# B transposed by the DMA engines, the state drive of chunk 0 moved behind its gate/up stage, and the down projections put behind the outputs of the chunk ahead, in a fused S5 and SwiGLU kernel

## The chip, the cores and the metric

One Trainium2 chip, one core of it. The metric is the device time of one execution in microseconds (us). Lower is better. A kernel is called faster or slower from 2% on.

Names of engines: PE is TensorE, PEld its weight loads, DVE is VectorE, ACT is ScalarE, POOL is GpSimd and SP is SyncE. A "q" behind a name (ACTq, SPq) marks a DMA issue in that engine's queue. L12 is line 12 of the kernel at hand, so that the same function has different line numbers in different kernels.

## The reference

The input is x of 2048 tokens by 448 features in bf16. A layer norm feeds two branches: a linear recurrence with 448 complex states (S5), and a SwiGLU feed-forward of width 1792. The output joins them.

```python
def _A_ref(x, Lambda_re, Lambda_im, B_re, B_im, C_re, C_im, log_dt, Dskip):
    Lam = Lambda_re + 1j * Lambda_im
    Lam_bar = jnp.exp(jnp.exp(log_dt) * Lam)
    B_bar = ((Lam_bar - 1.0) / Lam)[:, None] * (B_re + 1j * B_im)
    Bu = jnp.einsum("bld,pd->blp", x + 0j, B_bar)
    # h[t] = Lam_bar * h[t-1] + Bu[t], for 2048 steps
    return 2.0 * jnp.einsum("blp,dp->bld", hseq, Cmat).real + x * Dskip

def _B_ref(x, w_gate, w_up, w_down):
    return (silu(x @ w_gate) * (x @ w_up)) @ w_down

xn = _layernorm(x)
out = x + _A_ref(xn, ...) * silu(_B_ref(xn, w_gate, w_up, w_down))
```

## The kernel before

The tokens go through in four chunks of 512 (W), each of four tiles of 128 (TQ). One chunk needs, in this order of dependence:

- **drive**: bu = xn times B (PE), then a row of DVE steps. They turn bu against the phase tables CT and ST, scan each state over time, and turn back. The results are H_re and H_im.
- **gate/up** (`gu`): 14 blocks of 128 columns of the two weight matrices, two blocks at a time. ACT empties each PSUM bank, DVE multiplies, and the product is Vt.
- **downs**: four down projections (PE), each followed by a silu on ACT, which gives `sg`.
- **outs**: four output sums y = H times C (PE), which DVE multiplies by sg and adds to x.

The DVE steps of the drive are put in a background list. `bg.run(budget)` issues a few of them, and `bg.finish(q)` issues all that are left of chunk q. In the traces ACT and DVE run their instructions in the order in which the program issues them (the prediction shows an `sg` held up to 68.32 us behind four copies), so these calls decide what stands ahead of what.

```python
def b_transpose(c, d, eng):              # B is loaded as it lies, then turned on PE
    tp = bank("tpb", BF16).rearrange("p (i w) -> p i w", i=2)
    for i in range(2):
        for k in (KF, *range(KF)):
            ...
            nc.tensor.transpose(tp[:, i, c0 : c0 + P], nat[:, c, k, blk(d + i)], Id[:])
    ...                                   # and copied to BT by ACT or DVE

def bu(q, ns, packed=False):              # products with B; ACT empties the banks
    ...
    if packed:                            # swaps the halves of the packed last block:
        turn_over(b1[:, KF, :], b0[:, KF, :])   # two copies of 64 x 512 on ACT

def c_weights(k):                         # scales C by the factors of B_bar: block k
    ...
    for i, (o, ho, u, v) in enumerate(to):
        nc.scalar.activation(tb, natC[h, 1, k, :], ACT.Copy, scale=v[h, k : k + 1])
        nc.vector.scalar_tensor_tensor(out=C2[ho, o, :], in0=natC[h, 0, k, :],
            scalar=u[h, k : k + 1], in1=tb, op0=ALU.mult, op1=ALU.subtract)

def ssm_steps(bg, q):                     # DVE: 6 steps, 7 scans, then
    ...
    step(KF, h1, b1, CT, ALU.mult); step(KF, "t", b0, ST, ALU.mult)
    step(KF, h1, h1, "t", ALU.add)
    step(KT, h0, b0, CT, ALU.mult); step(KT, "t", b1, ST, ALU.mult)
    step(KT, h0, h0, "t", ALU.subtract)   # the last one completes H_re
```

The order of the stages (hooks: what is issued behind the n-th pair of gate/up blocks):

```python
load_w(nc.sync, nc.sync, Wg, B_w_gate, 0, C0)     # C0 = 256
load_w(nc.scalar, nc.scalar, Wu, B_w_up, 0, C0)   # two loads issued by ACT
load_nat(0, A_B_re)
...
gu(0, bg, 2.0, {
    0: [*stats(4, 5, 6, 7), *sqrt(1), on(params_in), on(table_phase, 0)],
    1: [*bs(1), *rstd_of(1), *norms(4, 5, 6, 7), on(table_sin, 0)],
    2: [*transposes(4, 5, 6, 7), on(load_c), on(table_phase, 1), on(table_sin, 1),
        on(bu, 0, (0, 1)), on(table_phase, 2), on(table_sin, 2)],
    3: [on(bu, 0, (2,), True), on(table_phase, 3), on(table_sin, 3), on(params_fold)],
    4: [on(params_trig), on(ssm_steps, bg, 0)],
    5: [on(params_out)],
}, begun)
gu(1, bg, 0.9, {
    1: stats(8, 9),
    2: [*stats(10, 11), *sqrt(2), on(c_weights, 0)],
    3: [*rstd_of(2), *norms(8, 9), on(c_weights, 1)],
    4: [*norms(10, 11), *transposes(8, 9), on(c_weights, 2)],
    5: [*transposes(10, 11), on(c_weights, 3)],
})
drive(1, 4.8)
for q in range(NQ - 1):
    # downs(q) with bg.run(2.2) after each; bg.finish(q); outs(q)
    # then, where there is a chunk q+2: drive(q+2), gu(q+2)
    ...
```

## Time and profile before

| | before |
|---|---|
| median of 3 runs | 190.0 us |
| span of the profiled execution | 188.1 us |
| busy: PE, DVE, ACT | 97%, 85%, 56% |
| first gate/up matmul | 7.40 us |
| downs of chunk 0 begin (S in what follows) | 64.30 us |
| first output sum of chunk 0 (first y matmul) | 74.90 us |
| last step of H_re of chunk 0, start and duration | 71.18 us, 1.23 us |

The page cuts the span into 40 equal slices, here 4.7 us each. Each digit is a busy share in tenths; in the row PEclk it is the TensorE clock that was granted, in tenths of full speed. These are two rows of the kernel before:

```profile
DVE  4889995899999999989999899789369999789253
PEclk9999999999999999999999999999999999999999
```

The clock is at full speed throughout. DVE is nearly full from the eighth to the 25th slice, among others with the drive's steps, and has some room after that. PE's own row is in the prediction.

### The profile page before, as it was taken

The numbers are of one execution on the slowest core, as the hardware profiler recorded it, in microseconds if no ns is written. First come the engines' busy times: TensorE is split into PE (matmuls) and PEld (weight loads), VectorE is DVE, ScalarE is ACT, GpSimd is POOL, SyncE is SP. The second block draws the span as 40 slices with busy tenths as digits, with TensorE's granted clock in tenths as the row PEclk, the third lists the DMA queues.
The fourth block names the chain that finished last, engine by engine and source line by source line (L and its number), as shares of the span: only waits on it lengthen the run. The fifth ranks groups of instructions, "written<-read, shape, count | busy, mean of one in ns | idle before, by whom it ended". The sixth has DMA issues, their size and how long they took to land.

```text
span 188.1 us, 3787 instructions
## 1 busy us (share of the span) xinstructions
PE 182.1 (97%) x1512; PEld 93.9 (50%) x1512; DVE 160.3 (85%) x266; ACT 105.1 (56%) x201; POOL 11.2 (6%) x21
## 2 busy tenths in 40 slices
PE   7799999999999999999999999999999999999992
PEld 2575455555555555545444455545444445555551
DVE  4889995899999999989999899789369999789253
ACT  3278699939999871018878632108977552302100
POOL 6422100000020000000020000000000000000000
PEclk9999999999999999999999999999999999999999
DMA  5999997300012100011004000020000000020020
GB/s 152 340 378 383 378 177 144 74 3 2 3 28 56 31 0 0 0 54 51 0 3 97 14 3 0 3 84 15 2 0 3 0 0 0 3 73 24 0 78 24
DMA packets 21122, 12.61 MB, mean 67 GB/s; under 512 B 11120, under 2 KB 20080, under 8 KB 21104
## 3 DMA queue, kind: packets, MB, share of 16 engines
q1 hardware_dynamic: 20288, 12.05, 23.2%
q10 hardware_dynamic: 688, 0.31, 0.6%
q8 instruction: 12, 0.20, 0.5%
q14 instruction: 6, 0.05, 0.1%
q0 software_dynamic: 128, 0.00, 0.0%
HBM read 8.03 MB, written 1.84 MB: 52 GB/s over the span
## 4 chain that ended last, share of the span: by engine, by line
PE 84%; DVE 9%; ACT 3%; DMA 1%; issue 1%; POOL 0%; SPq 0%; DVEq 0%
PE hd L559 23%; PE gp L424 20%; PE up L424 19%; PE y L574 11%; PE pb L424 9%; PE y L580 2%; DVE st L230 1%; DMA x_all<-in_A_x_dram 1%; DVE xn L248 1%; DVE f L356 1%; DVE a L357 1%; ACT CT L306 1%; DVE Vt L551 1%; ACT bu_im L458 1%; ACT bu_re L458 1%; DVE mv L231 1%
## 5 line engine op out<-in xcount | busy, mean ns | idle before, releaser
L424 PE MATMUL gp<-xT,Wg 64*128 64x512 bf16 (+1 forms) x406 | 86.2, 369 | 0.1
L424 PE MATMUL up<-xT,Wu 64*128 64x512 bf16 (+1 forms) x406 | 85.8, 369 | 0.1
L424 PEld LDWEIGHTS <-Wg 64*128 64x128 bf16 x406 | 36.9, 94 | 23.0 <-issue 1.6
L424 PEld LDWEIGHTS <-Wu 64*128 64x128 bf16 x406 | 37.2, 94 | 20.1 <-POOLq L406 0.3
L559 PE MATMUL hd<-Wd,Vt 128*128 128x448 bf16 x224 | 43.2, 353 | 0.0
L546 ACT ACTIVATE gs<-gp 128x512 bf16<-128x512 f32 x56 | 34.9, 623 | 12.4 <-PE gp L424 9.0
L547 ACT ACTIVATE us<-up 128x512 bf16<-128x512 f32 x56 | 35.2, 629 | 0.0
L559 PEld LDWEIGHTS <-Vt 128*128 128x128 bf16 x224 | 21.7, 98 | 21.0 <-issue 1.1
L564 ACT ACTIVATE sg<-hd 128x448 bf16<-128x448 f32 x16 | 8.7, 544 | 38.2 <-PE hd L559 38.2
L424 PE MATMUL pb<-xT,BT 64*128 64x512 bf16 (+1 forms) x224 | 22.0, 349 | 0.0
L551 DVE TENSOR_TENSOR Vt<-gs,us 128x2048 bf16<-128x2048 bf16 (+1 forms) x16 | 17.3, 1081 | 5.5 <-ACT us L547 5.4
L458 ACT ACTIVATE bu_re<-pb 128x512 bf16<-128x512 f32 (+1 forms) x20 | 10.0, 526 | 18.1 <-PE pb L424 18.1
L590 DVE TENSOR_TENSOR t<-y,sg 128x448 f32<-128x448 f32 (+2 forms) x17 | 10.1, 595 | 10.4 <-PE y L574 10.0
L574 PE MATMUL y<-C,H_re 128*128 128x448 bf16 (+2 forms) x68 | 17.6, 341 | 0.0
L424 PEld LDWEIGHTS <-BT 64*128 64x128 bf16 x224 | 11.2, 94 | 11.0 <-issue 0.7
L494 DVE TENSOR_TENSOR_SCAN bu_re<-rcol,H_re,ere 128x512 bf16<-128x512 f32 x12 | 15.1, 1269 | 0.0
L580 PE MATMUL y<-Dd,xT 128*128 128x128 bf16 x64 | 13.5, 212 | 0.0
L574 PE MATMUL y<-C,H_im 128*128 128x448 bf16 (+2 forms) x51 | 11.9, 342 | 0.0
L494 DVE TENSOR_TENSOR_SCAN bu_im<-rcol,H_im,eim 128x512 bf16<-128x512 f32 x9 | 11.3, 1260 | 0.0
L230 DVE BATCH_NORM_STATS2 st<-x_all 128x6 f32<-128x448 bf16 x16 | 9.9, 616 | 1.6 <-DMA x_all<-in_A_x_dram 1.5
L593 DVE TENSOR_TENSOR ob<-t,x_all 128x448 bf16<-128x448 f32 (+2 forms) x17 | 10.2, 597 | 0.6
L215 POOL TENSOR_TENSOR sd<-vep,halves 128x1 bf16<-128x1 bf16 (+1 forms) x7 | 5.9, 845 | 77.0 <-PE up L424 41.6
(90 smaller groups left out, 166.6 us busy)
## 6 DMA issues: line engine op xcount, KB each, us to landing
out_dram<-ob SPq DMA_DIRECT2D x15, 112.0 KB, 1.7
Wd<-in_B_w_down_dram SPq DMA_DIRECT2D x1, 1568.0 KB, 12.6
x_all<-in_A_x_dram SPq DMA_DIRECT2D x1, 896.0 KB, 14.5
Wg<-in_B_w_gate_dram SPq DMA_DIRECT2D x1, 768.0 KB, 8.2
Wu<-in_B_w_up_dram SPq DMA_DIRECT2D x1, 768.0 KB, 9.3
x_all<-in_A_x_dram SPq DMA_DIRECT2D x1, 448.0 KB, 5.1
Wg<-in_B_w_gate_dram SPq DMA_DIRECT2D x1, 384.0 KB, 4.9
Wu<-in_B_w_up_dram SPq DMA_DIRECT2D x1, 384.0 KB, 5.1
```

Source lines behind the costliest of these rows:

```text
L230: nc.vector.bn_stats(out=st[:], in_=x_all[:, n, :])
L424: mm = nc.tensor.matmul(out, lhsT=w[h, d, :], rhs=xT[h, d, q * W + c0 : q * W + c1], start=(first and m == 0), stop=(not first and m == 3 ...
L458: nc.scalar.activation(to, pair[i][0], ACT.Copy)
L494: nc.vector.tensor_tensor_scan(out=T["b"][c][:, k, :], data0=rcol[:, k : k + 1].to_broadcast([P, W]), data1=T["e"][c][:, k, :], initial=in ...
L546: nc.scalar.activation(gs[:, i + j, :], gp_[:], ACT.Silu)
L547: nc.scalar.activation(us[:, i + j, :], up_[:], ACT.Copy)
L551: nc.vector.tensor_tensor(out=Vt[:, f0 : f0 + n, :], in0=gs[:, 0:n, :], in1=us[:, 0:n, :], op=ALU.mult)
L559: nc.tensor.matmul(hd, lhsT=Vt_of[q][:, fi, j * P : (j + 1) * P], rhs=Wd[:, fi, :], start=(fi == 0), stop=(fi == NF - 1),)
L574: nc.tensor.matmul(y[:, c0:c1], lhsT=h, rhs=C2[:, n, c0:c1], start=(n == 0), stop=(n == NS - 1))
L580: nc.tensor.matmul(y[:, s + skip : s + P], lhsT=xT[:, n, m * P : (m + 1) * P], rhs=Dd[:, n, skip:P], start=False, stop=False,)
L590: nc.vector.tensor_tensor(out=t[:], in0=y, in1=sg[:, c0:c1], op=ALU.mult)
L593: nc.vector.tensor_tensor(out=ob[:], in0=t[:], in1=x_all[:, m, c0:c1], op=ALU.add)
```

## The change

Its intent, as the diff shows it:

1. **B turned by DMAs.** Six transposing loads write BT straight from memory, so the 32 PE transposes and their copies go. The loads wait (an empty instruction on SyncE) until Wu's columns up to 1280 have landed.
2. **Left halves of three blocks first.** The first 256 tokens are multiplied by three gate/up blocks, not two, before the next tokens are transposed. The added columns are loaded early, two of the parts being issued by ACT. DVE, no longer ACT, reads the `up` banks of the first pair.
3. **Drive 0 behind gate/up 0**, where its products with B stood inside gate/up 0 before.
4. **Down projections behind the outputs of the chunk ahead.** For the later chunks gate/up now comes between the downs and the outputs. Half of the scaling of C (blocks 2 and 3) and the layer norm of tiles 8 to 11 move out of gate/up 1 and in among the downs and outputs of chunk 0.
5. A root by the power of -0.5 in place of a power of 0.5 and a reciprocal.

```diff
+    def load_b(landed):
+        gate = nc.sync.nop(nofuse=True)
+        tc.add_manual_dep(gate.ins, landed.ins.name, SYNC, reason="queue")
+        load_turned(BT, A_B_re, 0, D)
+        load_turned(BT, A_B_im[KF * P : D, :], D, R)
+        load_turned(BT, A_B_im[0 : KF * P, :], KT * P, KF * P)
...
-    C0 = 256
+    C0, C1 = 256, 384
...
+    load_w(Wu, B_w_up, 0, C0, nc.scalar)
     load_x(2, TQ)
+    load_w(Wg, B_w_gate, 0, C0)
+    for part in range(2):
+        load_w(Wg, B_w_gate, C0, C1, nc.sync, part)
+        load_w(Wu, B_w_up, C0, C1, nc.scalar, part)
...
+    def second_tokens():
+        ln_evacuate(2, ln_transpose(2), nc.scalar)
+        t = ln_transpose(3)
+        tv = params_row(t)
+        ln_evacuate(3, t, nc.vector)
+        nc.scalar.activation(pcol[:], tv, ACT.Copy)
...
+    first, third = gu_banks(), gu_banks(1)
+    gu_matmuls(0, 0, first, (0, CW))
...
+    gu_matmuls(0, 2, third, (0, CW), between=second_tokens)
...
+    gu(0, bg, 0.0, {
+        0: [*stats(4, 5), on(params_in), on(table_phase, 0)],
+        2: [*stats(6, 7), *root(1), on(table_sin, 0)],
+        3: norms(4, 5, 6, 7),
+        4: [*transposes(4, 5, 6, 7), on(load_rest), on(table_phase, 1)],
+        5: [on(table_sin, 1), on(table_phase, 2)],
+        6: [on(table_sin, 2), on(table_phase, 3), on(params_fold), on(table_sin, 3),
+            on(params_trig)],
+    }, {0: first_pair, 1: second_pair})
+    drive(0, 0.0)
+    gu(1, bg, 1.6, {2: [on(c_weights, 0)], 4: [on(c_weights, 1)]})
     drive(1, 4.8)
...
+    sg = downs(0, 1.4, {
+        0: [on(c_weights, 2)],
+        1: [on(c_weights, 3), *stats(8, 9)],
+        2: [*stats(10, 11), *root(2), run_power],
+    })
+    bg.finish(0)
+    do(norms(8, 9) + transposes(8, 9))
+    outs(0, sg, {1: norms(10, 11) + transposes(10, 11)})
+    sg = downs(1, 2.5)
+    drive(2, 4.8)
+    gu(2, bg, 1.6, {...})
+    bg.finish(1)
+    outs(1, sg)
+    sg = downs(2, 2.5)
+    drive(3, 4.8)
+    gu(3, bg, 2.3)
+    bg.finish(2)
+    outs(2, sg)
...
```

## The prediction

> **What bounds the kernel now.** I read the busy shares first, then the slices.
>
> ```profile
> PE 182.1 (97%) x1512; PEld 93.9 (50%) x1512; DVE 160.3 (85%) x266; ACT 105.1 (56%) x201; POOL 11.2 (6%) x21
> PE   7799999999999999999999999999999999999992
> ```
>
> TensorE (PE) works from the third slice to the last but one, so only work taken off it or waits on it can move the time. Busy time hides short waits; so I went through the timeline by start-to-start distances. From the first real matmul at 7.40 us to the last near 184.5 us nearly every matmul starts when the array is free; all the gaps together are about 2 us. The largest gap, about 0.8 us, lies at 27.6 to 29.3 us, where ScalarE (ACT) was late emptying PSUM banks. The 32 transposes of B stand on PE too (grouped view by shape: columns are line, engine, form, count, then busy us and mean ns).
>
> ```profile
> L371 PE MATMUL tpb<-Id,nat 128*128 128x128 bf16 x32 | 2.1, 219 | 0.0
> L488 DVE TENSOR_TENSOR H_re<-H_re,tmp 128x2048 bf16<-128x2048 bf16 x4 | 4.9, 1224 | 0.1
> L389 DVE SCALAR_TENSOR_TENSOR C<-natC,nb_im,c_tb 128x448 bf16<-128x448 bf16 x3 | 2.0, 680 | 0.0
> ```
>
> They start 62 ns apart: two lots of 16 take 0.99 and 1.00 us. The next view is of the stretch in which the down projections of chunk 0 run, then its outputs (columns: us, then busy us of PE, PEld, VectorE (DVE), ACT, POOL).
>
> ```profile
> 64.30:74.90 10.60, 10.60 (x58) 5.49 (x57) 10.50 (x12) 5.56 (x11) 0.00 (x0) 1.00 0.01 2
> 74.90:81.08 6.18, 6.18 (x45) 3.43 (x45) 6.06 (x7) 0.54 (x1) 0.00 (x0) 1.00 0.00 0
> ```
>
> DVE is full there as well. It is the second engine, and what it delivers, H of chunk 0, is what the outputs read. The timeline shows the margin (start, us, instruction):
>
> ```profile
> 65.75 2.55 ACT L465 ACTIVATE bu_im<-bu_re 64x512 bf16<-64x512 bf16 x4
> 68.32 0.55 ACT L564 ACTIVATE sg<-hd 128x448 bf16<-128x448 f32 x1
> ...
> 71.18 1.23 DVE L488 TENSOR_TENSOR H_re<-H_re,tmp 128x2048 bf16<-128x2048 bf16 x1
> ```
>
> H_re is done at 72.4 us and PE wants it at 74.9: 2.5 us to spare. Note also ACT: the first sg is read only at 68.32, 4.0 us after the downs began, though its sum was ready at 66.95, because four copies of bu stood ahead of it in ACT's queue.
>
> **What the Trainium skill says.** (1) "TensorE: Matmul & The Clock Gate", Back-to-back issue gap: N/2.4 + 2.5 ns when warm. The trace agrees: 56 matmuls of 448 columns in 10.60 us are 189 ns each. (2) The same page, Architectural detail: ACT and DVE queues are strict first in, first out. The late sg above agrees, and my main step rests on it. (3) The same page, Part 1: a TensorE idle for one window of some 3.4 us can fall to half clock, and needs about as long to recover. The trace shows the half rate at the start only (dummy matmuls of 448 columns 0.37 us apart), no fall later, as PE never idles so long. (4) "DMA: Bandwidth & Descriptors", DMA Transpose (X-bar): 2-byte types, from Sync or Scalar, beside ordinary DMAs. Here a transposing load of C took 3.9 us to land, and SyncE some 1.3 us to issue.
>
> **The change, part by part.** I call S the moment at which the down projections of chunk 0 begin (64.3 before). Everything ahead of S first.
>
> - Start. ACT now issues four weight loads ahead of its first evacuation. The compiled order shows the fourth waiting for a DMA semaphore last used by the left 192 KB of Wg. Those landed 4.3 us after their issue at 2.13, so 6.4. The issue takes 0.45, and only then can ACT empty the two transposes of x:
>
> ```profile
> 5.96 0.60 ACT L261 ACTIVATE xT<-tp 128x512 bf16<-128x512 bf16 x1 [3.73 <-PE tp L259]
> 6.76 0.60 ACT L261 ACTIVATE xT<-tp 128x512 bf16<-128x512 bf16 x1 [0.20 <-PE tp L259]
> ```
>
>  They move to about 7.0 and 7.5, and the first matmul from 7.40 to 8.15: **+0.75**. The power of -0.5 saves a reciprocal (0.16) that no longer matters.
> - B by DMA: **-1.99** on PE, the 0.99 and 1.00 above. The six loads wait until Wu's columns up to 1280 have landed, about 14 us; six issues of 1.3 and 3.9 to land give about 26, and they are wanted at about 30.6: hidden.
> - Left half of the third block: no matmul more or less in all. It covers the transposes, but the copy of xT waits behind six parameter transposes in its bank, and the six matmuls left (0.33 us) cover it only in part: **+0.3**.
> - Drive 0 behind gate/up 0: the gap of 27.6 to 29.3 goes, **-0.8**. In its place ACT has the last two tables (1.15 us each, waiting for DVE's phases, 2.4 each) ahead of bu's evacuations. By my walk through both queues the first bank is free 0.65 us after PE wants it for gate/up 1: **+0.65**.
>
> Sum before S: 0.75 - 1.99 + 0.3 - 0.8 + 0.65 = **-1.1**; S is about 63.2.
>
> After S. PE runs four downs, 4 x 2.65 = 10.6 us, then asks for H of chunk 0. The compiled order says what DVE must do first. The third column pair of C stands before the last steps of H, and reads c_tb, which ACT makes behind the first sg. As before, the four copies hold sg to S + 4.0. Then sg 0.5 and c_tb 0.7: S + 5.2. From there DVE has, at start-to-start times of the trace: 4 scalings of C at 0.6 = 2.4; the last H_im step 0.95; LayerNorm statistics of tiles 8 to 11 at 0.94 = 3.76 (they now stand in front of H); H_re 1.15 + 1.25 + 1.2 = 3.6. Together 10.7, so H is ready at S + 15.9, and PE waits 15.9 - 10.6 = 5.3 us. Were c_tb not held up by the copies it would still be S + 4.0 + 10.7, a wait of 4.1. DVE gets to that point at about S + 2.6 in my walk, so its earlier load does not decide. I take **+5.2**. This wait is longer than 3.4 us: if the clock falls, some 3.4 us run at half rate and lose 1.7. I put that at one half, **+0.8**.
>
> Later chunks: their outputs come a whole gate/up stage (21.2 us) after the drive and downs, so DVE is ahead of them; the last H is ready about 1.2 us before its outputs. Nothing more or less there, and the tail is unchanged.
>
> Sum: -1.1 + 5.2 + 0.8 = +4.9; 190.0 + 4.9 = **194.9 us**.
>
> **The rivals.** First, that the wait at the outputs of chunk 0 is not there, because DVE or ACT are sooner than I count. Then only the part before S stays: 190.0 - 1.1 = 188.9, or 187.5 if the start is not held up either. For it: the author chose budgets for DVE's steps, and without idling DVE would need 33 us of the 34.5 between bu 0 and the outputs. Against it: the order of the queues is compiled, and the sum after c_tb is of measured durations. Second, that ACT becomes the bound around bu 0 (tables, eight bank reads and two copies in a row): the +0.65 could be 2 us, and the time 196.3. The gaps at 28 us before speak for it; that ACT is busy only 56% speaks against it. Third, that loads of 256-byte rows come too late for the third block, another 0.5 to 1 us: 195.5. The 16 engines are full from 5 to 20 us, so this is possible; but those loads replace larger ones of B at the same place. Fourth, no clock fall: 194.1.
>
> **Range and chances.** Sizes of the wait from 4.1 to 5.6, of the clock 0 to 1.7, of the part before S from -2.3 to +0.5 give 191.8 to 197 at the ends. I take 191.5 to 197.0. Slower by 2% begins at 193.8, which my sum passes by 1.1 only, and the first rival is a whole different outcome: slower 0.67, same 0.30, faster 0.03. Faster by 2% (186.2) would need 3.8 us, more than all gaps and transposes of B.
>
> **What would show it.** The changed profile should have: no tpb rows; the first gate/up matmul near 8.1, with an ACT issue of Wu at about 6.4 right before xT; a short PE gap at the first gate/up 1 matmuls, released by ACT; and one PE gap of 4 to 5.5 us at the first y matmul, released by DVE H_re, with DVE idle before C waiting for ACT c_tb. Half rate would show as y matmuls of 448 columns 0.37 apart after it. I am wrong if PE goes from downs to outputs of chunk 0 without a gap, if H_re is late for some other reason, or if a gap opens at a later chunk.

## The result

| | before | after |
|---|---|---|
| median | 190.05 us | 195.89 us |
| all runs | 189.99 to 190.41 (4) | 195.63 to 196.09 (4) |
| first gate/up matmul | 7.40 | 7.71 |
| S, downs of chunk 0 begin | 64.30 | 62.83 |
| first y matmul | 74.90 | 78.90 |
| outputs of chunk 0 take | 6.18 | 7.96 |

The ratio is 1.0302, with a 95% interval of 1.0285 to 1.032: slower. Ratios are the mean time of one kernel's fast runs over that of the other's in the same rounds, so they are not quite the ratio of the medians quoted. A run is called slow when it is over 1.5% above the fastest of its kernel, and is then left out of the ratio.

The busy shares and slices of the kernel after (a slice is now 4.86 us):

```profile
PE 182.3 (94%) x1493; PEld 93.1 (48%) x1493; DVE 160.1 (82%) x259; ACT 102.2 (53%) x197; POOL 11.7 (6%) x21
PE   7799999999999991799999999999999999999991
DVE  4659799774999499789999799799998599999453
PEclk9999999999999998599999999999999999999999
```

PE has a hole in one place only: the digit 1, slice 16. The clock is below full speed in that slice and in the next. The waits of PE (columns: who waits for whom, then us in total, times, longest) name the cause of the hole:

```profile
PE y L566 <- DVE H_re L475: 5.3, 1, 5.3
...
PE gp L412 <- ACT xT L267: 0.9, 1, 0.9
```

One wait of 5.3 us, at the first y matmul of chunk 0, for H_re. Now the same stretch in the timelines of ACT and DVE (start, us, instruction; in brackets the idle time before it and who ended it):

```profile
64.28 2.55 ACT L452 ACTIVATE bu_im<-bu_re 64x512 bf16<-64x512 bf16 x4
66.85 0.54 ACT L556 ACTIVATE sg<-hd 128x448 bf16<-128x448 f32 x1
67.29 0.66 ACT L378 ACTIVATE c_tb<-natC,b_re 128x448 f32<-128x448 bf16 x1
```

```profile
64.36 0.95 DVE L475 TENSOR_TENSOR tmp<-bu_re,ST 128x1536 bf16<-128x1536 bf16 x1
67.98 0.69 DVE L379 SCALAR_TENSOR_TENSOR C<-natC,nb_im,c_tb 128x448 bf16<-128x448 bf16 x1 [2.67 <-ACT c_tb L378]
...
71.59 0.63 DVE L235 BATCH_NORM_STATS2 st<-x_all 128x6 f32<-128x448 bf16 x1
...
73.48 1.22 DVE L475 TENSOR_TENSOR H_re<-bu_re,CT 128x2048 bf16<-128x2048 bf16 x1
...
77.63 1.22 DVE L475 TENSOR_TENSOR H_re<-H_re,tmp 128x2048 bf16<-128x2048 bf16 x1
```

Read them from left to right. ACT makes four copies of bu for chunk 1, then sg, then the c_tb that DVE needs. DVE stands idle for 2.67 us at the head of its queue, at the scaling of C, with steps of H behind it that could run. Then it does the rest of the scaling of C and the statistics of tiles 8 to 11, and only at 77.63 the last step of H_re. Before, that step stood at 71.18.

The first y matmuls after the wait run at half rate. The timeline of PE after shows starts 0.47 us apart for a y matmul with its Dd matmul, and from about 82.8 us the usual 0.25:

```profile
79.36 0.58 PE L566 MATMUL y<-C,H_re 128*128 128x448 bf16 x1
79.73 0.31 PE L572 MATMUL y<-Dd,xT 128*128 128x128 bf16 x1
79.83 0.58 PE L566 MATMUL y<-C,H_re 128*128 128x448 bf16 x1
...
82.78 0.35 PE L566 MATMUL y<-C,H_re 128*128 128x448 bf16 x1
...
83.03 0.35 PE L566 MATMUL y<-C,H_re 128*128 128x448 bf16 x1
```

The whole stage in one line each (columns: stretch, us, then the busy time of PE, PEld, DVE, ACT and POOL, the granted clock, the DMA share and GB/s). First the downs, then the outputs of chunk 0:

```profile
62.83:73.43 10.60, 10.60 (x57) 5.39 (x56) 7.66 (x14) 7.78 (x15) 0.00 (x0) 1.00 0.01 2
78.90:86.86 7.96, 7.96 (x45) 4.22 (x46) 6.17 (x14) 0.00 (x0) 0.81 (x1) 0.76 0.25 62
```

The downs take 10.60 us as before. DVE, though, is busy for 7.66 us of them where it was busy for 10.50: the 2.67 us of idling is nearly all the difference. The outputs take 7.96 us at a clock of 0.76, against 6.18 at 1.00.

So the account is S -1.5, wait +5.3, half rate +1.8. The sum is +5.6, and the medians differ by 5.8. In the two profiled runs nearly all of the difference can be placed. From S to the first y matmul it is 16.07 us against 10.60, that is +5.5: counted from start to start the wait is a little longer than the idle time. Behind the outputs of chunk 0 the rest takes 107.4 us against 107.0, +0.4, for a reason that stays open. The time outside the span is 1.8 us against 2.1, -0.3.

### The profile page after: what moved, and what is told of

Same layout as the page of the kernel before. It is cut to its first block, busy times and chain, and to the rows that moved or that the text cites. A ratio compares the mean times of both kernels' runs of the same rounds, so it can differ in the third digit from the quotient of the medians.

```text
span 194.3 us, 3749 instructions
## 1 busy us (share of the span) xinstructions
PE 182.3 (94%) x1493; PEld 93.1 (48%) x1493; DVE 160.1 (82%) x259; ACT 102.2 (53%) x197; POOL 11.7 (6%) x21
## 4 chain that ended last, share of the span: by engine, by line
PE 80%; ACT 7%; DVE 7%; DMA 2%; SPq 1%; issue 1%; ACTq 0%; DVEq 0%
PE gp L412 23%; PE up L412 19%; PE hd L551 16%; PE y L566 12%; PE pb L412 8%; DMA Wg<-in_B_w_gate_dram 2%; PE y L572 2%; DVE C L379 1%; ACT bu_im L452 1%; DVE st L235 1%; DVE H_re L475 1%; ACT gs L535 1%; ACT us L539 1%; ACT ST L311 1%; ACT bu_re L445 1%; ACT CT L312 1%
## 5 line engine op out<-in xcount | busy, mean ns | idle before, releaser
L412 PEld LDWEIGHTS <-Wg 64*128 64x128 bf16 x413 | 37.9, 94 | 23.4 <-issue 1.0
L412 PEld LDWEIGHTS <-Wu 64*128 64x128 bf16 x413 | 37.9, 94 | 20.6 <-issue 1.0
L535 ACT ACTIVATE gs<-gp 128x512 bf16<-128x512 f32 x56 | 33.8, 605 | 17.6 <-PE gp L412 17.5
L539 ACT ACTIVATE us<-up 128x512 bf16<-128x512 f32 x54 | 33.0, 610 | 0.0
L566 PE MATMUL y<-C,H_re 128*128 128x448 bf16 (+2 forms) x68 | 18.9, 361 | 5.3 <-DVE H_re L475 5.3
L566 PEld LDWEIGHTS <-H_re 128*128 128x128 bf16 x68 | 6.9, 102 | 12.7 <-DVE H_re L475 5.7
L566 PE MATMUL y<-C,H_im 128*128 128x448 bf16 (+2 forms) x51 | 12.4, 355 | 0.0
L221 POOL TENSOR_TENSOR rstd<-vep,halves 128x1 f32<-128x1 f32 (+1 forms) x7 | 6.2, 892 | 93.7 <-DVE vep L237 61.0
```

What stands on the lines that cost most here:

```text
L412: mm = nc.tensor.matmul(out, lhsT=w[h, d, :], rhs=xT[h, d, q * W + c0 : q * W + c1], start=(first and m == 0), stop=(not first and m == 3 ...
L535: nc.scalar.activation(gs[:, i + j, :], gp_[:], ACT.Silu)
L539: nc.scalar.activation(us[:, i + j, :], up_[:], ACT.Copy)
L566: nc.tensor.matmul(y[:, c0:c1], lhsT=h, rhs=C2[:, n, c0:c1], start=(n == 0), stop=(n == NS - 1))
```

## The experiments

**Theory.** DVE's queue in the downs of chunk 0 sets the end. It carries two things that stood in gate/up 1 before: half of the scaling of C, held up by ACT, and the statistics of tiles 8 to 11. Each takes its own share of the wait. The clock then falls as a consequence of the wait. **Rivals:** H is late for some other reason (such as the late drive itself), in which case moving these two would leave the wait in place; or the half rate is no cost of its own, because the stretch is bound by DVE anyway. The part before S is tested as well.

The first four kernels below are the changed kernel with one edit each, the third with the first two edits together. They ran together on one chip, with the kernel before at 190.12 us in the same rounds.

### Statistics of tiles 8 to 11 out of the way

```diff
-        1: [on(c_weights, 3), *stats(8, 9)],
-        2: [*stats(10, 11), *root(2), run_power],
+        1: [on(c_weights, 3)],
     })
     bg.finish(0)
-    do(norms(8, 9) + transposes(8, 9))
-    outs(0, sg, {1: norms(10, 11) + transposes(10, 11)})
+    outs(0, sg, {
+        0: stats(8, 9),
+        1: [*stats(10, 11), *root(2), run_power],
+        2: norms(8, 9) + transposes(8, 9),
+        3: norms(10, 11) + transposes(10, 11),
+    })
```

> The changed kernel with one move: the LayerNorm statistics of tiles 8 to 11 (and their root and norms) stand behind the outputs of chunk 0 instead of in front of the last steps of H. Theory A (queue order): H_re comes 4 x 0.94 = 3.76 us sooner, at about 75.1 us; the wait of PE at the first y falls from 5.3 to about 1.6 us, too short for the clock to fall, so 1.9 us of slow matmuls go as well: about 190.2 us. Rival B (VectorE is simply overloaded): the wait comes back at the outputs of a later chunk, and the time stays above 192. Rival C (the slow matmuls are not due to idling): 195.9 - 3.7 = 192.2, with y matmuls still 0.37 us apart.

Measured: 191.2 us (190.95 to 191.46), ratio 1.0051 (1.0034 to 1.0067). The waits of PE:

```profile
PE y L566 <- DVE H_re L475: 1.6, 1, 1.6
...
PE pb L412 <- DMA xT<-xn: 0.5, 1, 0.5
```

The wait fell by 3.7 us, from 5.3 to 1.6, to the tenth as expected, and the clock did not fall (0.996 to 0.999). The time is 1 us above what I expected, and half of that is the second line; the other half is not located. The norms of tiles 8 to 11 now come so late that the transposing DMAs of chunk 2 arrive after PE asks for them. That is a side effect of my edit, not of the change.

### Scaling of C out of the way

```diff
-    gu(1, bg, 1.6, {2: [on(c_weights, 0)], 4: [on(c_weights, 1)]})
+    gu(1, bg, 1.6, {2 + k: [on(c_weights, k)] for k in range(KT)})
...
-        0: [on(c_weights, 2)],
-        1: [on(c_weights, 3), *stats(8, 9)],
+        1: [*stats(8, 9)],
```

> The changed kernel with one move: the four scalings of C stand behind blocks 2, 3, 4 and 5 of gate/up 1 (as in the kernel before) instead of two there and two behind the downs of chunk 0. Theory A: VectorE no longer waits 2.7 us for c_tb behind the first sg, but does 2.4 us of scaling in time in which it was partly idle; H_re at about 76.1 us in place of 78.9, the wait of PE about 2.6 us, no clock fall: about 191.2 us. Rival B (overload): the 2.4 us of work are only moved, H_re stays later than 78 us, and the time stays at 195 to 196.

Measured: 193.03 us (192.01 to 193.11), ratio 1.013 (1.0098 to 1.0162). The wait is as expected, the time is not. The waits and the timeline of PE:

```profile
PE y L566 <- DVE H_re L475: 2.6, 1, 2.6
```

```profile
76.07 0.37 PE L566 MATMUL y<-C,H_re 128*128 128x448 bf16 x1 [2.65 <-DVE H_re L475]
76.27 0.27 PE L572 MATMUL y<-Dd,xT 128*128 128x128 bf16 x1
76.33 0.58 PE L566 MATMUL y<-C,H_re 128*128 128x448 bf16 x1
```

The first pair of matmuls runs at full rate (0.26 us from y to y), and from 76.33 on each takes almost twice as long: the clock fell after an idle time of 2.65 us. Three of the four runs have a mean clock of 0.987 to 0.991 and 193.0 to 193.1 us; the fourth has 1.0 and 192.01 us. So the miss is mostly the clock, which I had thought safe below 3.4 us. The fourth run is still 0.8 above what I expected, and what that is stays open.

### Both out of the way

The two edits above together.

> Both moves together. Theory A: H_re at about 72.3 us, 1.1 us before PE asks for it; no wait and no clock fall: 195.9 - 5.4 - 1.9 = 188.6 us, and this beats the kernel before by about 0.7%. Rival B (overload): a wait of 1 to 4 us opens at the outputs of chunk 1 or of chunk 3, and the time is 190 or more.

Measured: 189.78 us (189.48 to 190.12), ratio 0.9977 (0.9957 to 0.9996). No wait at y is left. The last step of H_re is now at 71.11 us (77.63 in the kernel after), and a wait for the transposing DMAs of chunk 2 is there instead:

```profile
71.11 1.23 DVE L475 TENSOR_TENSOR H_re<-H_re,tmp 128x2048 bf16<-128x2048 bf16 x1
```

```profile
PE pb L412 <- DMA xT<-xn: 1.0, 1, 1.0
```

With both moved nothing of the wait is left, though drive 0 is as late as in the kernel after. Whether an earlier drive 0 would have hidden these two is not tested. Most of what is over the expected 188.6 is this 1.0 us, again from moving the norms too far back.

### The wait filled with work, the wait left in place

```diff
     do(norms(8, 9) + transposes(8, 9))
+    warm(28)
     outs(0, sg, {1: norms(10, 11) + transposes(10, 11)})
```

28 matmuls whose result is used by nothing keep PE busy for about as long as it would wait.

> The changed kernel with 28 dummy matmuls of 448 columns (5.3 us) on PE where it waits for H of chunk 0; H_re is no sooner. It measures the clock alone. Theory A (idling halves the clock): y matmuls follow 0.19 us apart and the time is 195.9 - 1.9 = 194.0 us. Rival C (the y matmuls are slow for another reason): the time stays at 195.9 and the y matmuls 0.37 us apart.

Measured: 194.19 us (194.09 to 194.34), ratio 1.0209 (1.0193 to 1.0224), clock 0.996 to 1.0. The first y matmul is at 78.79 us, where it was at 78.90, so the wait itself is unchanged; but the outputs run at full rate:

```profile
73.31 5.46 PE L179 MATMUL warm<-Wd 128*128 128x448 bf16 x28
78.79 0.36 PE L566 MATMUL y<-C,H_re 128*128 128x448 bf16 x1
...
79.05 0.35 PE L566 MATMUL y<-C,H_re 128*128 128x448 bf16 x1
```

The half rate alone therefore costs 195.89 - 194.19 = 1.7 us, and it is a cost of its own: DVE does not hold those outputs back.

### B by DMAs alone, in the kernel before

The next four ran together on one chip, with the kernel before at 190.03 us. This one starts from the kernel before and takes part 1 of the change only; nothing else is moved. The loads of B wait here for Wu's columns up to 768, not 1280.

```diff
-    load_nat(0, A_B_re)
     load_x(TQ, 2 * TQ)
-    load_gu(C0, 768)
-    load_nat(1, A_B_im)
+    landed = load_gu(C0, 768)
     load_gu(768, F)
+    load_b(landed)
...
-    for d in range(0, KT, 2):
-        b_transpose(0, d, nc.scalar)
...
-        1: [*bs(1), *rstd_of(1), *norms(4, 5, 6, 7), on(table_sin, 0)],
+        1: [*rstd_of(1), *norms(4, 5, 6, 7), on(table_sin, 0)],
```

> The kernel before with one part of the change alone: B turned by six DMAs behind Wu's columns up to 768, and no transposes of B on PE. Theory A (32 transposes of 62 ns are PE time): the second 16 give back their 1.00 us in full; the first 16 stood where PE waits for the copies of xT anyhow (9.9 to 10.65 us), so they give back only some 0.25. About 190.1 - 1.25 = 188.9 us, if the six loads land before bu 0 asks for B at about 24.5 us. Rival: they land too late (first issue about 12.5 us, six issues of 1.3 us, 3.9 us to land: 24.3 us) and PE waits for them: 189.5 or more. Full gain of 1.99 us: 188.1.

Measured: 191.98, 192.2, 193.78 and 195.12 us, the last slow; ratio 1.0135 (1.0088 to 1.0182) from the fast ones. The waits of PE:

```profile
PE pb L407 <- DMA BT<-in_A_B_im_dram: 2.9, 1, 2.9
...
PE gp L407 <- DVE xT L264: 0.6, 1, 0.6
PE pb L407 <- DMA BT<-in_A_B_re_dram: 0.4, 1, 0.4
```

A miss, and the mistake was mine. In the order of before PE asks for B at about 18.5 us (the first product starts at 18.89 after waiting 0.4), not at the 24.5 us that I had taken. The six loads are issued from 10.9 to 21.0 us and PE waits 3.3 us for them. It also shows that the first half of the transposes of B filled a time in which PE would have waited for xT (0.6 us). The runs differ more than usual: mean clocks of 1.0, 1.0, 0.991 and 0.979. The half rate is likely to be in the two slower ones, but the run that was profiled is one with 1.0, so no trace shows it. With the loads placed so, turning B by DMA does not pay in the old order. In the change the drive stands behind gate/up 0: there the loads are issued from 16.2 to 24.1 us and no wait for BT shows.

### ACT's late issue at the start

```diff
         load_w(Wg, B_w_gate, C0, C1, nc.sync, part)
-        load_w(Wu, B_w_up, C0, C1, nc.scalar, part)
+        load_w(Wu, B_w_up, C0, C1, nc.sync, part)
```

In the kernel after, the fourth issue of ACT stands ahead of the reads of the transposed tokens (the timeline of ACT after):

```profile
3.74 0.40 ACTq L143 DMA_DIRECT2D Wu<-in_B_w_up_dram  x1
6.19 0.34 ACTq L148 DMA_DIRECT2D Wu<-in_B_w_up_dram  x1
6.57 1.08 ACT L267 ACTIVATE xT<-tp 128x512 bf16<-128x512 bf16 x2 [4.34 <-PE tp L261]
```

> The changed kernel with the loads of Wu's columns 256 to 384 issued by SyncE behind those of Wg, not by ScalarE. Theory A (ScalarE's fourth DMA issue holds up its first evacuation): xT is read at 5.7 and 6.5 us, the first gate/up matmul starts at about 7.15 in place of 7.71 us, and everything after it moves with it: 195.9 - 0.5 = 195.4 us. Rival: the first matmuls wait for the weights instead, and the time stays at 195.9.

Measured: 195.92 us (195.43 to 196.5), ratio 1.0309 (1.0282 to 1.0335). In the trace the first gate/up matmul moved from 7.71 to 7.09 us and S from 62.83 to 62.23 us, as expected, and the wait at y is 5.3 us as before. In the time nothing shows. The reason lies in the half rate: in the profiled run the y matmuls are slow from 78.30 to about 83.8 us, against 78.90 to about 82.7 in the kernel after, and the outputs of chunk 0 take 8.78 us against 7.96. The 0.62 us is itself a comparison of single traces: in seven others whose start is that of the kernel after, the first gate/up matmul stands at 7.46 to 7.98 us. The runs fall into two groups, 195.4 to 195.6 us at a clock of 0.991 and 196.3 to 196.5 us at 0.979 and 0.982. A comparison to half a microsecond is not possible on top of that; the mechanism is shown by the trace, its worth in time by no run of this kernel.

### The norms one output sooner

```diff
     bg.finish(0)
+    do(stats(8, 9))
     outs(0, sg, {
-        0: stats(8, 9),
-        1: [*stats(10, 11), *root(2), run_power],
-        2: norms(8, 9) + transposes(8, 9),
-        3: norms(10, 11) + transposes(10, 11),
+        0: [*stats(10, 11), *root(2), run_power],
+        1: norms(8, 9) + transposes(8, 9),
+        2: norms(10, 11) + transposes(10, 11),
     })
```

The kernel with both moved, with its own side effect mended.

> Both moves of the third run, with the norms of tiles 8 to 11 one output sooner, so that the transposing DMAs of xT land before bu 2 asks for them (there PE waited 1.0 us for them). Theory A: that wait goes and no other comes: 189.8 - 1.0 = 188.7 us. Rival: VectorE is then late with the reads of y, or H of a later chunk: 189.5 or more.

Measured: 188.61 us (188.43 to 188.91), ratio 0.9924 (0.991 to 0.9939), clock 0.997 to 1.0. Neither the wait at y nor that for xT is left. H_re is complete at 72.7 us and PE asks for it at 73.61. Below before by 1.4 us: about what S gained (1.47 in the kernel after, 1.29 in this one). The kernel beats both others, clear of the noise, but by less than the 2% from which it would be called faster.

### The order of the later downs undone

The kernel just shown, with the downs of chunk 2 put back behind gate/up 3.

```diff
     outs(1, sg)
-    sg = downs(2, 2.5)
     drive(3, 4.8)
     gu(3, bg, 2.3)
+    sg = downs(2, 2.5)
     bg.finish(2)
```

> The seventh kernel (e7_fixed) with one part of the change undone for the later half: the downs of chunk 2 again directly ahead of their outputs, behind gate/up 3, not ahead of drive 3. Theory A: PE has the same work and VectorE is ahead of it in either order, so the same within 0.3 us as e7_fixed, about 188.7. Rival (the new order is what keeps VectorE ahead): a wait at the outputs of chunk 2 or 3 and 189.5 or more.

Measured: 188.65 us (188.41 to 188.94), ratio 0.9926 (0.9909 to 0.9942). That the downs of chunk 2 stand ahead of gate/up 3 is worth nothing here: where DVE is not late, PE has the same work in either order.

### Three small things at the start

On top of the mended kernel: Wu's added parts issued by SyncE; the six small transposes of the parameters put ahead of the first gate/up stage, into a bank of their own, in place of the two dummy matmuls.

```diff
-        load_w(Wu, B_w_up, C0, C1, nc.scalar, part)
+        load_w(Wu, B_w_up, C0, C1, nc.sync, part)
...
-        warm(1 + n)
+        if n == 0:
+            warm(1)
+    tv = params_row(bank("tv", BF16))
```

> e7_fixed with three small things at the start: Wu's second parts issued by SyncE instead of ScalarE, so that no issue waits ahead of the reads of the transposed tokens; the six parameter transposes put ahead of the first gate/up stage, in PE time that is idle anyway, instead of ahead of the first B product; no dummy burst there. Theory (each is on PE's path to the start of the down projections, and after e7 nothing behind it waits): -0.55 for the start (as e6_start's trace showed), -0.25 for the copy of the transposed tokens that came late behind the parameter transposes, -0.38 for the transposes themselves: about 187.5 us, clock 0.99 or more, ratio about 0.987. Rival (the gain is eaten by a slower clock, because fewer PE operations come before the first stage, or by the next wait down the line): 188.6 as e7_fixed.

Measured: 188.93 us (188.75 to 189.39), ratio 0.9934 (0.9921 to 0.9948). A miss; the rival's 188.6 is nearer. Of its two reasons the second is what shows, the next wait down the line; the clock, at 0.995 to 1.0, is hardly slower. The first gate/up matmul did come sooner, at 7.28 us, but the timeline of PE shows a new wait at the second four transposes of tokens:

```profile
9.36 0.40 PE L261 MATMUL tp<-Id,xn 128*128 128x128 bf16 x4
10.44 0.38 PE L261 MATMUL tp<-Id,xn 128*128 128x128 bf16 x4 [0.69 <-ACT xT L267]
```

The eight PSUM banks go round in the order of allocation. Counting them, the transposes of tile 3 now get the bank of the parameters. Its read, `pcol`, stood in ACT's queue behind the read of tile 2.

### The read of that bank moved up

```diff
     tv = params_row(bank("tv", BF16))
+    nc.scalar.activation(pcol[:], tv, ACT.Copy)
...
-        nc.scalar.activation(pcol[:], tv, ACT.Copy)
```

> e9_best with ScalarE's read of the parameter bank (pcol) moved up, right behind the parameter transposes. In e9_best the transposes of token tile 3 waited 0.7 us; counting the banks in the order of their allocation, they got the bank of the parameters, whose only read stood in ScalarE's queue behind the read of tile 2. Theory (that read released the bank): no wait at those transposes, the down projections of chunk 0 start about 0.6 us sooner than in e9_best, and the time is about 0.5 us below e7_fixed run beside it, ratio to before about 0.990. Rival (the clock or the next wait eats it): a wait of about the same size moves to the first products of the third block's right half, and the time is that of e7_fixed.

> e7_fixed once more, unchanged, beside e10_read on the same chip, so that the two can be compared to a few tenths of a us: 0.9924 times the kernel before, as it was, or 188.6 us.

Measured, on one chip: 188.57 us (187.95 to 189.41), ratio 0.9914 (0.9895 to 0.9932), for the read moved up; 188.88 us (188.64 to 189.45), ratio 0.9928 (0.9914 to 0.9942), for the mended kernel run again beside it. All eight transposes now run without a break:

```profile
9.41 0.62 PE L261 MATMUL tp<-Id,xn 128*128 128x128 bf16 x8
```

S is at 62.07 us, against 63.19 with the wait, so the cause of the wait is shown; the 1.1 us between these two traces is more than the wait alone. The time is 0.3 us below the mended kernel by the medians. The two intervals overlap: whether these three small things together are worth more than nothing in time is not settled.

## Why the prediction was right

The predicted time was 194.9 us with a range of 191.5 to 197.0, and it was called slower. Measured were 195.89 us, slower. By its own steps:

- **Start, predicted +0.75.** Measured +0.31: the first gate/up matmul moved from 7.40 to 7.71 us. The mechanism was right, as the kernel with SyncE's issues showed by bringing it to 7.09. The size was off for two reasons in the trace (a single one; the spread of the start is given at the experiment): the fourth issue was done at 6.53, not 6.85, and both reads of xT followed as one pair within 1.08 us.
- **B, predicted -1.99 and hidden.** The transposes are gone and no wait for BT shows. The experiment on the kernel before adds that it was not so with the drive at its old place: there PE waited 3.3 us for them.
- **Third block, predicted +0.3.** A gap of 0.25 us, behind the matmuls that start at 10.95 us.
- **Drive 0, predicted -0.8 and +0.65.** The gap ahead of 29.3 us is gone; one of about 0.55 us is at 35.4 to 36.9 us. But from the first gate/up matmul to S PE now takes 55.12 us in place of 56.90, 1.78 less. With 1.99 less for B and 0.25 more for the third block, next to nothing is left for the drive: the gap moved and did not shrink. The prediction had 0.15 less in all.
- **S, predicted 63.2.** Measured 62.83; most of the difference is the start.
- **The wait at y, predicted +5.2.** Measured 5.3, and along the chain that the prediction walked: sg at S + 4.0, DVE idle until c_tb is made, the last H_re ready at S + 16.0. The two moved kernels took out 3.7 us and 2.7 us of it, and together all of it. This is shown.
- **The clock, predicted +0.8.** This is the term that was mis-sized. It was 1.7 us taken at a chance of one half. The size was right (1.7 us by the kernel with the wait filled; 1.8 us by the duration of the outputs), the chance was not: every run of the kernel after has a mean clock of 0.982 or 0.991, where the runs of before beside the experiments have 0.996 or more. Had I taken it whole, the sum would have been 195.8.
- **Later chunks, predicted 0.** Measured +0.4 us behind the outputs of chunk 0, unexplained.

Three sums in the prediction are slips. The upper ends that it names give 190.0 + 0.5 + 5.6 + 1.7 = 197.8, not 197. The first rival without the held-up start is 188.9 - 0.75 = 188.15; for 187.5 the +0.65 has to go too. And the 3.8 us that "faster" would need are not more than all gaps and transposes of B (2 and 1.99 us), but about as much.

Of the rivals, the first (no wait there) describes the mended kernel: it gave 188.9 for that case, and 188.61 was measured. The second, ACT as the bound around bu 0, and the third, loads too late for the third block, did not show. The fourth, no clock fall, is what the filled kernel brought about on purpose: 194.1 was given, 194.19 measured.

The third citation of the prediction, on the clock, served well as a warning but badly as a limit. The kernel with C out of the way went to half rate after 2.65 us of idling in the profiled run, and in three of four runs by the mean clock. A wait of 1.6 us left the clock alone in all four runs, and so did the 2.9 us for BT in the profiled run of B by DMAs alone. The granted clock of short stretches shows what the mean hides (columns as for the stretches above; two lines of the kernel after, then two of the kernel with C out of the way):

```profile
72.49:75.90 3.41, 1.10 (x6) 0.39 (x4) 3.34 (x7) 0.55 (x1) 0.00 (x0) 1.00 0.00 0
75.90:82.73 6.83, 3.83 (x15) 1.83 (x16) 5.60 (x13) 0.00 (x0) 1.92 (x1) 0.50 0.09 19
72.88:76.30 3.42, 0.77 (x5) 0.24 (x4) 3.28 (x9) 0.54 (x1) 1.34 (x1) 1.00 0.00 0
76.30:79.71 3.41, 3.41 (x15) 1.63 (x14) 2.43 (x6) 0.00 (x0) 0.58 (x1) 0.50 0.19 38
```

The half rate lasts 6.83 us in the one and 3.41 us in the other, and 6.82 us (76.98 to 83.80) with SyncE's issues: two, one and two times the window of the page. In the kernel after it begins 2.3 us after the last down projection ended, and 3.0 us of it lie within the wait. In the 3.41 us ahead of the fall PE was still busy for 1.10, 0.77 and 0.00 us. Each trace also keeps the times at which the granted clock changed. Counted on from the first of them in steps of 3.41 us, the falls stand at the end of a step. In the traces of the two waits that left the clock alone no step has less than 1.75 us of PE work, and the 2.9 us are shared by two steps. So what counts seems to be how a wait lies in these steps, and not its length alone. That is a reading of five traces; no run moved a wait within the steps.

## What to carry to other kernels

When a stage is moved later to close one gap, list what else its engines have to deliver until its consumer asks. Here a gap of less than 1 us on TensorE was to be closed and one of 5.3 us opened, because VectorE's queue still held a scaling that waited for ScalarE, and statistics that nobody needed yet, ahead of the step that TensorE did need. In an engine that works in order, put work with a late consumer behind the step with an early one, but measure how far back it may go: moved one output too far, it cost another 1.0 us. And reckon with a half rate behind a wait of TensorE of 2.6 us or more: here it lengthened the outputs by 1.7 to 2.6 us in three traces (7.77, 7.96 and 8.78 us, where 6.1 to 6.2 is usual), and a fourth trace, with a wait of 2.9 us, has none.

## What the Trainium skill lacked or had wrong

- "TensorE: Matmul & The Clock Gate", Part 1: it has the clock fall after an idle window of some 3.4 us and calls the window free-running. The length agrees: the half rate lasted 6.83, 3.41 and 6.82 us in three profiled runs. (Estimates from the mean clocks of 0.991 and 0.982 agree too: 0.009 x 194.3 / 0.5 = 3.5 us and 0.018 x 194.3 / 0.5 = 7.0 us.) What it does not say is how idle a window has to be. Here PE was still busy for 1.10 and 0.77 us of the 3.41 us ahead of two falls, and 1.75 us or more of work left the clock alone in two other traces. So an idle time of 2.65 us was enough in one profiled run (mean clock 0.987 to 0.991 in three of four runs), and 2.9 us was not in another; 1.6 us was not in four runs (0.996 to 0.999).
- "DMA: Bandwidth & Descriptors", DMA Transpose (X-bar): it lists what such a load may be. Bandwidths stand elsewhere in the skill, but I found no time for the issue of one such load or for the landing of one of this size. The loads of B took about 1.3 us each to issue on SyncE and 3.7 to 4.0 us (median) from issue to landing.
- No page that I read gives the price of a DMA issue that waits in a computing engine's queue: ACT's fourth issue started 2.45 us after its third and was done at 6.53 us, and two reads of PSUM stood behind it; with the issues on SyncE the first gate/up matmul came 0.62 us sooner (7.09 us, against 7.46 to 7.98 in eight traces with the issue on ACT).
